# A retention and gated-convolution kernel: a loop in code and rotating tile pools, and one written list of small steps on fixed buffers

## Chip, cores and metric

The kernel runs on one core of a Trainium2 chip. The metric is the device time in microseconds (us). TensorE (PE) multiplies, VectorE (DVE), ScalarE (ACT) and GpSimd (POOL) work on tiles, SyncE (SP) issues the transfers. Each engine takes its instructions in the order in which the program gives them. TensorE writes into PSUM, eight banks of 512 float32 columns on 128 partitions.

## The reference, cut to what matters

```python
# q, k, v: (8, 8, 576, 64): batch, heads, tokens, head size; float32
scores = q @ k.T / 8                         # per batch and head
ret = scores * gamma[h] ** (i - j) where i >= j, else 0
x = (ret @ v), heads side by side            # (8, 576, 512)
gate_pre[t] = sum over kk of conv_w[kk] * x[t - 4 + kk]   # 5 taps per channel, causal
gate = 1 / (1 + exp(-gate_pre))
val = x @ w_val                              # 512 x 512
out = (gate * val) @ w_out                   # 512 x 512
```

## The kernel before

The decay factors out: k-side tokens are weighted with gamma^-j by multiplying v (`gin`), query tokens with gamma^i and the 1/8 when x is taken (`gout`). Causality is then a plain mask, and what earlier tokens give to later ones is a 64x64 state per head, which is carried.

The 576 tokens of a batch are cut into two units of 256 (two chunks c of 128 tokens) and a rest of 64; the rests of four batches make one unit more. That gives 18 units (`units`, L69), the last two being the rests. A partition holds two neighbouring tokens (r = 2). Per unit, in the names of the code:

- `load` (L97) brings k, q and v in quarter-megabyte halves by SP, in runs of 512 bytes; four buffers each. `cast1` (L212) makes bf16 on POOL (in the first units also on ACT and DVE) and weights v.
- `turn` (L231) transposes k and q, 16 transposes of 128x128 on TensorE, and `take_turn` (L248) copies them to SBUF on ACT.
- `scores` (L259) makes k q^T in two halves of 16 matmuls, each on a 64x64 part of the array (`QUAD`, L76, names the four parts), and `masks` (L273) multiplies by the mask on DVE.
- `carried` (L294) adds state times q, `values` (L322) adds v times masked scores, in the same two banks; `take_x` (L334) multiplies by `gout` into `xg` on DVE.
- `update` (L353) makes k^T v for the state, ACT copies it, and POOL adds it up (L378 to L394).
- `conv` (L417) does the five taps as 40 matmuls of 64x64 diagonal blocks by 256 tokens, in two banks; `gates` (L431) is the sigmoid on ACT.
- `value` (L440) does x w_val, 16 matmuls of 128x128 by 256 tokens, and `gated` (L450) multiplies by the gate on DVE.
- `project` (L456) does z w_out, 8 matmuls of 512 columns; ACT copies; `store` (L466) writes out by SP.

The order is written by hand from L490 to L609 for the units 0 to 3, with dummy matmuls (`warm`, L204) between; from L610 on, one loop does unit n's attention and unit n-1's convolution, values and projection:

```python
scores(n, 0); masks(n, 0)
conv(n - 1, 0)
carried(n, 0)
scores(n, 1, lambda: carried(n, 1)); masks(n, 1)
gate_values(n - 1, 0); gate_values(n - 1, 1)
values(n, 1); values(n, 0); take_x(n)
update(n + 1); cast(n + 2); turn(n + 1, ps_a)
take_turn(n + 1, 0); take_turn(n + 1, 1)
rows_out(n - 1)
```

Buffers come from pools that rotate. PSUM has four pools of two banks: `ps_a` (turns, convolution), `ps_s` (scores, update), `ps_o` (carried and values), `ps_v` (values of x, projection).

Of the kernel before, what the change touches and what calls it, by code (L numbers as in the profile page):

```python
# [16 lines left out]
PSUM = bass.MemoryType.PSUM  # L18


@with_exitstack
def kernel(
# [16 lines left out]
    NCH = S // P  # L39
    TAIL = S - NCH * P  # L40
    PAD = KC - 1
    GB = 4
    LA = 6
    W = 2 * P
    NC2 = S // W
    assert D == 64 and DM == H * D and TAIL == 64 and B % GB == 0 and NP == 4
    scale = 1.0 / math.sqrt(D)
    lng = [math.log(1.0 - 2.0 ** (-5.0 - h)) for h in range(H)]

    consts = ctx.enter_context(tc.tile_pool(name="c", bufs=1))  # L50
    lead = consts.tile([P, 96], F32, name="lead")
    ldp = ctx.enter_context(tc.tile_pool(name="ld", bufs=4))
    bfp = ctx.enter_context(tc.tile_pool(name="bfp", bufs=3))
    tp_sb = ctx.enter_context(tc.tile_pool(name="tsb", bufs=2))
    pp = ctx.enter_context(tc.tile_pool(name="pp", bufs=1))
    gp = ctx.enter_context(tc.tile_pool(name="gp", bufs=1))
    zp = ctx.enter_context(tc.tile_pool(name="zp", bufs=2))
    op_sb = ctx.enter_context(tc.tile_pool(name="osb", bufs=2))
    stp = ctx.enter_context(tc.tile_pool(name="stp", bufs=2))
    xp = ctx.enter_context(tc.tile_pool(name="xp", bufs=1))  # L60
    small = ctx.enter_context(tc.tile_pool(name="small", bufs=1))
    ps_a = ctx.enter_context(tc.tile_pool(name="psa", bufs=1, space=PSUM))
    ps_s = ctx.enter_context(tc.tile_pool(name="pss", bufs=1, space=PSUM))
    ps_o = ctx.enter_context(tc.tile_pool(name="pso", bufs=1, space=PSUM))
    ps_v = ctx.enter_context(tc.tile_pool(name="psv", bufs=2, space=PSUM))
# [5 lines left out]
    NU = len(units)  # L71

    jobs = [(u,) for u in range(NU)]
    lo, hi = slice(0, 64), slice(64, 128)
    half = (lo, hi)
    QUAD = ((0, 0), (1, 1), (0, 1), (1, 0))  # L76

    with tc.manual_schedule():

        loaded = {}  # L80
        SRC = {"k": k, "q": q, "v": v}

        def load1(n, u):
            kind, b, c = units[u]
            src = SRC[n]
            t = ldp.tile([P, H, 2 * D], F32, name=f"f{n}c")
            if kind == "full":
                for h0 in range(0, H, H // 2):
                    hs = slice(h0, h0 + H // 2)
                    nc.sync.dma_start(out=t[:, hs], in_=src[b, hs, c * W:(c + 1) * W, :].rearrange("h (p r) d -> p h (r d)", r=2))  # L90
            else:
                for i in range(GB):
                    nc.sync.dma_start(out=t[i * 32:(i + 1) * 32],
                                      in_=src[b + i, :, NC2 * W:S, :].rearrange("h (p r) d -> p h (r d)", r=2))
            loaded[n, u] = t

        def load(u):  # L97
            for n in "kqv":
                load1(n, u)

        nc.gpsimd.memset(lead[0:1, 0:1], 0.0)
        load(0)
        cwn = consts.tile([KC * NP, P], F32, name="cwn")
        nc.scalar.dma_start(out=cwn, in_=moe_conv_w.rearrange("k (o i) -> (k o) i", i=P))
        wvf = consts.tile([P, NP, DM], F32, name="wvf")
        wof = consts.tile([P, NP, DM], F32, name="wof")
        load(1)
        nc.sync.dma_start(out=wvf, in_=moe_w_val.rearrange("(o i) n -> i o n", i=P))
        wo_src = moe_w_out.rearrange("(pr ab hl p) n -> ab hl p pr n", pr=2, ab=2, hl=2)
        for (p0, blk, ab, hl) in ((0, 0, 0, 0), (64, 0, 1, 0), (0, 2, 1, 1), (64, 2, 0, 1)):  # L110
            nc.sync.dma_start(out=wof[p0:p0 + 64, blk:blk + 2, :], in_=wo_src[ab, hl])
        for u in range(2, 5):
            load(u)


        zero = consts.tile([P, 512], BF16, name="zero")
        nc.vector.memset(zero, 0.0)
        lsc = small.tile([P, 1], F32, name="lsc")
        lcol = small.tile([P, NP], F32, name="lcol")
        nc.vector.memset(lsc, math.log(scale))  # L120
        for h in range(H):
            nc.vector.memset(lcol[half[h % 2], h // 2:h // 2 + 1], lng[h])
        ident = small.tile([P, P], BF16, name="ident")
        nc.gpsimd.memset(ident, 1.0)
        nc.gpsimd.affine_select(ident, ident, pattern=[[-1, P]], base=0, channel_multiplier=1,
                                compare_op=ALU.is_equal, fill=0.0)
        identf = small.tile([32, 32], F32, name="identf")
        nc.vector.tensor_copy(identf, ident[0:32, 0:32])
        id2 = small.tile([P, 64], F32, name="id2")
        nc.vector.tensor_tensor(id2, ident[:, 0:64], ident[:, 64:128], op=ALU.add)  # L130

        posi = small.tile([P, S], mybir.dt.int32, name="posi")
        for c in range(2 * NC2):
            nc.gpsimd.iota(posi[:, c * P:(c + 1) * P].rearrange("p (r a) -> p r a", r=2), pattern=[[1, 2], [2, 64]],
                           base=c * P, channel_multiplier=0)
        nc.gpsimd.iota(posi[:, NC2 * W:S].rearrange("p (r a) -> p r a", r=2), pattern=[[1, 2], [2, 32]],
                       base=NC2 * W, channel_multiplier=0)
        toki = small.tile([P, NC2 + 1, 2], mybir.dt.int32, name="toki")
        nc.gpsimd.iota(toki[:, 0:NC2], pattern=[[W, NC2], [1, 2]], base=0, channel_multiplier=2)
        for i in range(GB):  # L140
            nc.gpsimd.iota(toki[i * 32:(i + 1) * 32, NC2, :], pattern=[[1, 2]], base=NC2 * W, channel_multiplier=2)
        gout = consts.tile([P, NP, S], F32, name="gout")

        def prep_gout(prs):
            for pr in prs:
                nc.scalar.activation(gout[:, pr, :], posi, AF.Exp, bias=lsc, scale=lcol[:, pr:pr + 1])

        tok = small.tile([P, NC2 + 1, 2], F32, name="tok")
        lrow = small.tile([P, H], F32, name="lrow")
        gin = small.tile([P, NC2 + 1, H, 2], F32, name="gin")  # L150
        for h in range(H):
            nc.vector.memset(lrow[:, h:h + 1], -lng[h])

        def prep_gin():
            nc.vector.tensor_copy(tok, toki)
            nc.vector.tensor_tensor(gin, tok.unsqueeze(2).to_broadcast([P, NC2 + 1, H, 2]),
                                    lrow.unsqueeze(1).unsqueeze(3).to_broadcast([P, NC2 + 1, H, 2]), op=ALU.mult)
            nc.scalar.activation(gin, gin, AF.Exp)


        mask = consts.tile([P, 2, P], BF16, name="mask")
        mask_h = consts.tile([P, 2, P], BF16, name="maskh")
        for (t, base) in ((mask, 0), (mask_h, P)):
            nc.gpsimd.memset(t, 1.0)
            nc.gpsimd.affine_select(t.rearrange("p j (r a) -> p j r a", r=2), t.rearrange("p j (r a) -> p j r a", r=2),
                                    pattern=[[-1, 2], [1, 2], [2, 64]], base=base, channel_multiplier=-2,
                                    compare_op=ALU.is_ge, fill=0.0)
        mask_t = consts.tile([P, 2, P], BF16, name="maskt")

        def prep_masks():  # L170
            nc.vector.tensor_copy(mask[hi], mask_h[hi])

        def prep_tail_mask():
            nc.vector.tensor_copy(mask_t, mask)
            for i in (0, 2):
                nc.vector.memset(mask_t[i * 32:i * 32 + 32].rearrange("p j (r a) -> p j r a", r=2)[:, :, :, 32:64], 0.0)

        xg = xp.tile([P, B, NP, PAD + S], BF16, name="xg")
        nc.gpsimd.memset(xg[:, :, :, 0:PAD], 0.0)

        wvb = consts.tile([P, NP, NP, P], BF16, name="wvb")
        wob = consts.tile([P, NP, DM], BF16, name="wob")
        dg = consts.tile([P, NP, KC, 64], BF16, name="dg")

        def prep_conv():
            cps = ps_a.tile([P, KC * NP], F32, name="a")
            nc.tensor.transpose(cps, cwn, identf[0:KC * NP, 0:KC * NP])
            cw = small.tile([P, KC * NP], F32, name="cw")
            nc.vector.tensor_copy(cw, cps)
            nc.vector.tensor_tensor(  # L190
                dg.rearrange("p o k j -> p k o j"),
                cw.rearrange("p (k o) -> p k o", o=NP).unsqueeze(3).to_broadcast([P, KC, NP, 64]),
# [473 lines left out]
```

## Time and profile before

| what | us |
|---|---|
| median of 3 runs (lowest, highest) | 168.03 (166.53, 168.66) |
| profiled execution, span from first to last instruction | 169.3 |
| busy PE, PE weight load, DVE, ACT, POOL in it | 150.8, 112.8, 99.6, 88.8, 98.4 |
| moved by DMA | 40.35 MB, mean 238 GB/s |

The profiled execution is one more execution; its span is its own time and lies 1.3 us above the median of the runs. In the slices of the profile the span is cut into 40 equal parts of 4.23 us, and a digit is the busy share in tenths; PEclk is the granted TensorE clock. In a chain line stand the start, the length, the engine and the line. In a group line stand the shape, the count, the busy us, the mean ns of one, and the idle time ahead of them with what ended it. Matmuls overlap in their pipeline, so the mean ns of a matmul is longer than the step from one to the next.

### The profile page before, as it was taken

To read this page: it belongs to the slowest core of one execution; us is meant where nothing else is said; L and a number is where in the kernel's file an instruction comes from. 1 tells how busy PE (TensorE), PEld (TensorE's weight loads), DVE (VectorE), ACT (ScalarE), POOL (GpSimd) and SP (SyncE) were. 2 spreads that over 40 slices of the span, in tenths; PEclk is the share of its full clock that TensorE was granted. 3 is DMA by queue.
4 is the path that set the end of the run, shared out by engine and by line. 5 is a ranking of instruction groups with operands and counts; after the bars stand their busy time and mean duration, and the time that the engine had idled before them with its cause. 6 is when DMAs were issued, how large, how long until landed. Compare 5 with 4: busy or idle time off the path is not lost.

```text
span 169.3 us, 7640 instructions
## 1 busy us (share of the span) xinstructions
PE 150.8 (89%) x3384; PEld 112.8 (67%) x3402; DVE 99.6 (59%) x153; ACT 88.8 (52%) x127; POOL 98.4 (58%) x123
## 2 busy tenths in 40 slices
PE   6677589978899979998999999999999999999960
PEld 2366456647678756877787776868787877868620
DVE  5684543475758481858383856658584938668330
ACT  6965330565273827382838374564838382654520
POOL 7565197157875846584849594956769499100000
PEclk9999755999999999999999999999999999999999
DMA  4999978999999999999999999787980311303125
GB/s 143 290 341 351 284 218 258 316 325 322 314 323 329 282 342 295 307 332 323 329 282 327 296 304 274 251 235 237 240 273 21 128 68 60 127 9 128 45 78 126
DMA packets 61071, 40.35 MB, mean 238 GB/s; under 512 B 2394, under 2 KB 57710, under 8 KB 61038
## 3 DMA queue, kind: packets, MB, share of 16 engines
q1 hardware_dynamic: 61008, 39.86, 77.7%
q8 instruction: 26, 0.43, 1.1%
q14 instruction: 7, 0.06, 0.1%
q10 hardware_dynamic: 30, 0.01, 0.0%
HBM read 30.42 MB, written 9.44 MB: 235 GB/s over the span
## 4 chain that ended last, share of the span: by engine, by line
PE 77%; DMA 5%; DVE 4%; issue 4%; POOL 4%; ACT 2%; SPq 1%; POOLq 0%; ACTq 0%; DVEq 0%
PE v L445 18%; PE v L461 17%; PE a L424 13%; PE a L246 8%; PE s L266 6%; PE o L330 6%; PE o L307 3%; DMA fqc<-in_q_dram 3%; PE s L367 2%; POOL vb L215 2%; DMA fkc<-in_k_dram 2%; DVE p L276 2%; SPq L90 1%; PE o L246 1%; DVE z L452 1%
## 5 line engine op out<-in xcount | busy, mean ns | idle before, releaser
L276 DVE TENSOR_TENSOR p<-s,mask 128x1024 bf16<-128x1024 f32 x28 | 34.3, 1224 | 40.2 <-PE s L266 40.2
L445 PE MATMUL v<-xg,wvb 128*128 128x256 bf16 x288 | 36.6, 281 | 0.5 <-DVE xg L341 0.5
L215 POOL TENSOR_TENSOR vb<-fvc,gin 128x1024 bf16<-128x1024 f32 x18 | 34.3, 1903 | 3.3 <-DMA fvc<-in_v_dram 3.3
L461 PE MATMUL v<-wob,z 128*128 128x512 bf16 x126 | 33.5, 380 | 1.3 <-DVE z L452 0.4
L249 ACT COPY kq<-a 128x1024 bf16<-128x1024 bf16 x28 | 27.0, 1015 | 10.0 <-PE a L246 10.0
L445 PEld LDWEIGHTS <-wvb 128*128 128x128 bf16 x288 | 27.3, 100 | 6.4 <-issue 1.4
L452 DVE TENSOR_TENSOR z<-gate,v 128x512 bf16<-128x512 f32 x36 | 24.6, 683 | 9.2 <-ACT gate L433 5.3
L433 ACT ACTIVATE gate<-a 128x1024 f32<-128x1024 f32 x18 | 18.4, 1024 | 16.1 <-PE a L424 9.1
L464 ACT COPY ob<-v 128x512 f32<-128x512 f32 x36 | 20.0, 605 | 9.6 <-PE v L461 9.6
L424 PE MATMUL a<-xg,dg 64*64 64x256 bf16 x720 | 24.2, 278 | 0.0
L375 ACT COPY xf<-s 128x512 f32<-128x512 f32 x12 | 7.0, 586 | 31.2 <-PE s L367 31.2
L341 DVE TENSOR_TENSOR xg<-o,gout 128x512 bf16<-128x512 f32 x32 | 22.2, 741 | 0.2
L461 PEld LDWEIGHTS <-z 128*128 128x128 bf16 x144 | 13.0, 98 | 13.6 <-DVE z L452 1.4
L424 PEld LDWEIGHTS <-dg 64*64 64x64 bf16 x720 | 20.5, 109 | 2.1 <-DVE xg L348 0.4
L266 PEld LDWEIGHTS <-kq 64*64 64x64 bf16 x576 | 13.5, 106 | 11.0 <-issue 10.0
L266 PE MATMUL s<-kq 64*64 64x128 bf16 x512 | 16.5, 223 | 3.2 <-issue 2.8
L389 POOL TENSOR_TENSOR mid<-run,xf 128x256 f32<-128x256 f32 x8 | 5.8, 727 | 20.3 <-ACT xf L375 14.2
L221 POOL CAST kb<-fkc 128x1024 bf16<-128x1024 f32 x16 | 16.6, 1039 | 0.2 <-DMA fkc<-in_k_dram 0.2
L221 POOL CAST qb<-fqc 128x1024 bf16<-128x1024 f32 x15 | 15.6, 1041 | 0.2 <-DMA fqc<-in_q_dram 0.2
L380 POOL CAST s<-xf 128x256 bf16<-128x256 f32 x8 | 3.2, 398 | 20.2 <-ACT xf L375 13.6
L330 PE MATMUL o<-p,vb 64*64 64x128 bf16 x576 | 12.6, 224 | 1.2 <-DVE p L276 1.2
L330 PEld LDWEIGHTS <-vb 64*64 64x64 bf16 x576 | 9.4, 109 | 5.3 <-issue 5.1
(75 smaller groups left out, 157.7 us busy)
## 6 DMA issues: line engine op xcount, KB each, us to landing
fkc<-in_k_dram SPq DMA_DIRECT2D x32, 256.0 KB, 5.1
fqc<-in_q_dram SPq DMA_DIRECT2D x32, 256.0 KB, 5.1
fvc<-in_v_dram SPq DMA_DIRECT2D x32, 256.0 KB, 5.1
out_dram<-ob SPq DMA_DIRECT2D x16, 512.0 KB, 4.8
wvf<-in_moe_w_val_dram SPq DMA_DIRECT2D x1, 1024.0 KB, 9.2
wof<-in_moe_w_out_dram SPq DMA_DIRECT2D x4, 256.0 KB, 10.0
fkc<-in_k_dram SPq DMA_DIRECT2D x8, 128.0 KB, 4.1
fqc<-in_q_dram SPq DMA_DIRECT2D x8, 128.0 KB, 4.5
```

The costliest lines, as they stand in the source:

```text
L215: nc.gpsimd.tensor_tensor(t.rearrange("p h r d -> p (h r) d"), loaded["v", u].rearrange("p h (r d) -> p (h r) d", r=2), gin[:, units[u][2] ...
L221: (eng or nc.gpsimd.tensor_copy)(t.rearrange("p r h d -> p h r d"), loaded[n, u].rearrange("p h (r d) -> p h r d", r=2))
L249: nc.scalar.copy(kqt[u][hf].rearrange("p i l r c a -> p i (l r c a)"), tps[u][:, :, hf].rearrange("p i l r a -> p i (l r a)"))
L266: nc.tensor.matmul(s[half[c], par, prl, r, :], lhsT=t[half[par], 0, prl, r, c, :], rhs=t[half[par], 1, prl, :, c, :], start=True, stop=Tru ...
L276: nc.vector.tensor_tensor(p.rearrange("p e l r a -> p (e l) (r a)"), sps[u, hf].rearrange("p e l r a -> p (e l) (r a)"), m.rearrange("p r ...
L330: nc.tensor.matmul(o[c][half[par], pr, :], lhsT=vb[half[c], 2 * pr + par, r, :], rhs=p[half[c], par, prl, r, :], start=first(u, c, par), s ...
L341: nc.vector.tensor_tensor(x[:, b, :, PAD + i0:PAD + i0 + P].rearrange("p o (a r) -> p o r a", r=2), o[c].rearrange("p o (r a) -> p o r a", ...
L424: nc.tensor.matmul(g[cols, bank, si, :], lhsT=dg[rows, blk, kk, :], rhs=xs(j, rows, blk, kk), start=(si == 0 and kk == 0), stop=(si == len ...
L445: nc.tensor.matmul(vp[:, si, :], lhsT=wvb[:, o, 2 * e + s, :], rhs=xs(j, slice(0, P), o, PAD), start=(si == 0 and o == 0), stop=(si == len ...
L452: nc.vector.tensor_tensor(zsb[j][:, 2 * e + ss[0]:2 * e + ss[-1] + 1, :], gsb[j, i][:, e], vps[j, i, e], op=ALU.mult)
L461: nc.tensor.matmul(o, lhsT=z[:, r, :], rhs=wob[:, jj, :], start=(jj == 0), stop=(jj == NP - 1))
L464: (eng or nc.scalar.copy)(outs[u][:, r], o)
```

## The change

The program becomes one list of 811 words, `ORDER`, which a last loop runs through; each word names a step, its unit or job, and its buffers or banks. There are no pools: every SBUF tile is a fixed buffer chosen by a number modulo its count, and PSUM is one tile of eight banks that the words name. The dummy matmuls shrink to three.

- Units stay; work behind x goes by jobs: units 0, 1, 16 and 17 alone, the others in pairs, so that `conv`, `sigmoid`, `value` and `gated` see 512 columns. `project` stays at one unit and one r.
- q is loaded per batch in halves of four heads (512 tokens, a partition holds four neighbouring tokens, runs of 1 KB; batch 0 by units). Tokens of a chunk then stand in the order of four, in q, masks, `gout` and x's PSUM columns.
- Turns work on row halves of 64 partitions and give 64 columns each.
- Convolution runs on 32x32 blocks, each row group into a bank of its own (four banks); the weights' rows and columns are laid out to match, and in odd pairs of heads the two halves of x's partitions change places.
- `carried` takes the tiles in an order in which four different parts of the array follow each other; there are no `fence` copies.
- Five buffers hold k and v (and in two of them first the weights), two hold q; three row buffers instead of two. The rests have their own x, `xt`, and `last_x` copies the four tokens that they need.
- Casts, copies and state steps name their engine in the list: 12 k casts, 6 q casts and 28 row copies go to ACT, 8 row copies and 8 turn copies to DVE, 45 of 48 state steps and 17 of 18 v casts to POOL.

The core of the diff:

```diff
+UNITS = [0, 1, 2, 3, 4, 5, 6, 7, 8, 9, 10, 11, 12, 13, 14, 15, 16, 17]
+JOBS = [(0,), (1,), (2, 3), (4, 5), (6, 7), (8, 9), (10, 11), (12, 13), (14, 15), (16,), (17,)]
+ORDER = """
...
+OC.4.0.0.6.A S.9.1.0.4 K.9.1.2 S.9.1.1.4 L.v.15.0 L.v.11.1 L.v.11.0 LQ.6.1 SS.9.2.P CK.11.2.P CQ.5.2.1.P CVV.11.2.P
+SS.10.1.P SS.10.0.P CQ.6.2.1.P PJ.4.1.1.7 PJ.4.0.1.6 X.8.0.0 X.8.1.0 M.9.1.4 PV.9.1.0.2 PV.9.0.0.2 K.9.0.2 PV.9.1.1.2
+PV.9.0.1.2 X.9.1.2 X.9.0.2 TK.10.0 TQ.5.2.4 OC.4.0.1.6.A OC.4.1.1.7.A TK.11.6 KT.10.0.A QT.5.1.5.A CV.5.0 QT.5.0.4.D
+KT.11.6.D SG.5.1.0 V.5.2.4 G.5.2.4 SG.5.0.0 S.10.1.0.6 K.10.1.2 S.10.1.1.6 M.10.1.6 S.10.0.1.4 S.10.0.0.4 M.10.0.4
...
+        def load_q(b, hh):
+            t = ldq[b % LOADQ].rearrange("p h r d -> p h (r d)")
+            nc.sync.dma_start(out=t[:, heads(hh)],
+                              in_=q[b, heads(hh), 0:NC2 * W, :].rearrange("h (p r) d -> p h (r d)", r=4))
...
+        def turn_k(i, b0):
+            ps = bank16[:, b0:b0 + 2].rearrange("p c (o r a) -> p c o r a", r=2, a=64)
+            for pr in range(NP):
                 for r in range(2):
+                    for c in range(2):
+                        nc.tensor.transpose(ps[:, c, pr, r, :],
+                                            kb[i % KBS][half[c], r, 2 * pr:2 * pr + 2, :].rearrange("p h d -> p (h d)"),
+                                            ident[half[c], half[c]])
...
+        def carried(i, odd, b0):
+            kind, b, cu = units[seq[i]]
+            for m in range(2):
+                for (prl, par) in ((0, 0), (1, 1), (1, 0), (0, 1)):
+                    pr, c, s = 2 * m + prl, par ^ odd, par ^ prl
                     rows = half[par]
+                    o = bank[half[s], b0 + c, pr * P:(pr + 1) * P]
...
+        def conv(j, b0):
+            n = cols(j)
+            for kk in range(KC):
+                for d in range(4):
+                    for rg in range(4):
+                        cg = (rg + d) % 4
+                        rows, cs = slice(32 * rg, 32 * rg + 32), slice(32 * cg, 32 * cg + 32)
+                        nc.tensor.matmul(bank[cs, b0 + rg, 0:n], lhsT=dg[rows, cg, kk, :], rhs=xs(j, rows, cg, kk),
+                                         start=(kk == 0), stop=(kk == KC - 1), skip_group_check=True)
...
+        def value(j, e, bk):
+            n = cols(j)
+            for o in range(NP):
+                nc.tensor.matmul(bank[:, bk, 0:n], lhsT=wvb[:, o, e, :], rhs=xs(j, slice(0, P), o, PAD),
+                                 start=(o == 0), stop=(o == NP - 1), skip_group_check=True)
...
+        for word in ORDER:
+            name, *args = word.split(".")
+            run[name](*args)
```

The words of the list are: L, LQ, LQ1, LQT, LV, LO, LC load k and v, q, and the weights; CK, CQ, CVV cast; TK and TQ turn, KT and QT copy the turns; S scores, M masks, K carried, PV weighted sums, X takes x; U update, XF its copy, SS the state's three steps; CV convolution, SG sigmoid, V values, G gating, PJ projection, OC its copy, ST store; XP copies the last tokens for the rests; words with z are set-up. A last letter A, D or P names the engine.

## The prediction

> **What bounds the kernel now.** I read the page's slices first, then the busy times by stretches of ten microseconds, then the chain that ended last, then the groups of instructions. The slices show two regimes.
>
> ```profile
> PE   6677589978899979998999999999999999999960
> DVE  5684543475758481858383856658584938668330
> PEclk9999755999999999999999999999999999999999
> DMA  4999978999999999999999999787980311303125
> ```
>
> Up to slice 11 (about 46 us) TensorE has holes and a stretch at half the granted clock; behind it TensorE is full to the last two slices. The DMA engines are full nearly from the start to about 105 us. The stretches say the same in numbers (busy us of PE, PEld, DVE, ACT and POOL, then granted clock, DMA share, GB/s):
>
> ```profile
> 20.00:30.00 10.00, 8.96 (x108) 6.22 (x108) 4.28 (x7) 3.06 (x7) 8.75 (x11) 0.55 0.87 252
> 40.00:50.00 10.00, 8.89 (x244) 6.69 (x245) 6.16 (x11) 5.21 (x11) 6.98 (x10) 1.00 1.05 323
> 90.00:100.00 10.00, 9.95 (x254) 7.77 (x254) 6.25 (x7) 6.34 (x9) 7.92 (x10) 1.00 1.03 311
> 100.00:110.00 10.00, 9.95 (x230) 7.94 (x227) 6.61 (x8) 5.54 (x7) 7.42 (x7) 1.00 0.85 269
> ```
>
> A busy TensorE alone proves little, so the chain decides. One turn of the steady loop, start and length in us:
>
> ```profile
> 95.34 0.28 PE s L367 x32
> 95.62 1.00 PE a L246 x16
> 96.62 0.22 PE v L461
> 96.89 1.46 PE v L461 x6
> 98.34 0.35 PE s L266 x16
> 98.69 1.23 PE a L424 x40
> 99.92 0.22 PE o L307 x4
> 100.46 0.17 PE s L266 x6
> 100.62 1.85 PE v L445 x16
> 102.48 0.57 PE o L330 x32
> 103.05 0.28 PE s L367 x32
> ```
>
> Nothing but TensorE stands in it: one unit costs 103.05 - 95.34 = 7.71 us. By starts: update 0.28, turns 1.00, projection 1.72, half of the scores 0.35, convolution 1.23, carried states with the other half of the scores 0.70 (so carried alone 0.35), values 1.85, weighted sums 0.57. Here TensorE work removed is time removed, until another engine takes over. The groups give the second in line, and three prices:
>
> ```profile
> L276 DVE TENSOR_TENSOR p<-s,mask 128x1024 bf16<-128x1024 f32 x28 | 34.3, 1224 | 40.2 <-PE s L266 40.2
> L452 DVE TENSOR_TENSOR z<-gate,v 128x512 bf16<-128x512 f32 x36 | 24.6, 683 | 9.2 <-ACT gate L433 5.3
> L341 DVE TENSOR_TENSOR xg<-o,gout 128x512 bf16<-128x512 f32 x32 | 22.2, 741 | 0.2
> ```
>
> DVE's masks wait for the scores, not the scores for the masks.
>
> **The change part by part**, per unit of 256 tokens, on TensorE.
>
> Convolution: 40 matmuls of 64x64 by 256 columns become 80 of 32x32 by 512 for two units. With four tiles abreast, 40 x 256 columns are 2560 column times in 1.23 us. With sixteen abreast, two units need 5 x 512 = 2560, so 1.23 us for two, 0.62 for one: 0.61 saved. Bounds: 0.35 (80 weight-and-matmul pairs for two units at the update's pace, 0.28 us / 32 = 8.75 ns, the fastest row) and 2.46 (still four abreast: 80 x 512 / 4 = 10240 columns for two units at 1.23 us per 2560, 4.9 us). I take 0.62, since the rows of 64x64 tiles run as wide as their array allows. For a job of one unit (four of them: 80 by 256 columns) I take half of the streaming and the same edge, 0.70, 0.53 saved.
>
> Against this speaks a rule of the Trainium skill, "TensorE: Matmul & The Clock Gate", Part 1: start to start never falls below about 25 ns. By it the 880 matmuls would take 22 us, as much as the old 18 x 1.23 = 22.1. The trace disagrees: L367 starts one per 8.75 ns.
>
> Turns: 16 transposes of 128 rows by 128 columns become 32 of 64 rows by 64 columns (16 for k, half of 32 for two units' q). If the two row halves run abreast, the columns in line fall from 2048 to 1024: 0.50. Bounds 0.28 (32 x 8.75 ns) and 2.00 (32 x 62.5 ns, each as long as now). I take 0.50, as L367 and L424 show both row halves at work together. Saved 0.50.
>
> Carried: the same 16 matmuls, but now four instead of two different tiles follow each other (the heads of odd pairs change halves). 0.35 becomes 0.18; bounds 0.14 (16 x 8.75) and 0.35. Saved 0.17.
>
> Values: 16 matmuls of 512 columns for two units instead of 32 of 256. Projection streams 512 columns in 1.72 / 8 = 215 ns, so 3.44 plus one edge of 0.14 for two, 1.78 for one: 0.07 saved. Bounds 1.72 and 1.85. Projection, scores, weighted sums and update keep their matmuls and tile sizes: nothing.
>
> Edges: each piece of the chain is 0.07 to 0.16 us longer than its columns need (weighted sums: 32 x 128 / 4 columns at the projection's 0.42 ns are 0.43, measured 0.57). The old loop changes tile size four times a unit, the list about 6.1 times from the turn of unit 4 on. 2.1 x 0.1 = 0.21 us lost per unit, bounds 0 and 0.34. Beside it stands the Trainium skill's "TensorEngine Tiling (Array Packing)", Key Properties, that a change of tiling mode drains the array; it gives no figure.
>
> Sum behind 46.5 us: turns 14 x 0.50 = 7.0, carried 14 x 0.17 = 2.4, convolution 13 x 0.61 + 2 x 0.53 = 9.0, values 13 x 0.07 = 0.9, edges -14 x 0.21 = -3.0. Together 16.3 us; a double unit's cost falls to 7.71 - 1.14 = 6.57.
>
> What lies beside. DVE keeps masks, gating and x: (34.3 + 4.9 + 4.9 + 24.6 + 22.2 + 3.0) / 18 = 5.2 us a unit. The list gives it 8 row copies, 8 turn copies and a few casts more, about 12 us or 0.7 a unit by the copies' rows (0.4 to 0.9 each). x is now written with a step of four elements; the step of two costs 741 - 683 = 58 ns over the plain write, so 0 to 58 more, twice a unit. 5.9 to 6.0 of 6.57: covered, but 90% full. If cover fails, at worst each unit waits for one mask, 1.22. ACT gains 12 k casts and 6 q casts (1.05 each, 19 us) and loses 16 copies: about 100 us in all, covered. POOL loses those casts (98.4 to about 87). Its queue reaches v sooner, which costs nothing.
>
> SP: q comes in halves of a batch, 1 KB runs instead of 512 B; about as many DMAs (some 140 for 150, about 0.5 us of issue each). Stores stand among loads in the list, so a store that waits for its copy holds the loads behind it; five key and value slots (four before) cover that by some 6 us each. Fixed banks: the convolution holds four of eight until two sigmoids of 1.02 are through, 3.2 us in 13.1 of a pair. The other four carry turns, scores and weighted sums; I price it at nothing, covered by the list's putting values behind it, at worst 1.02 per pair.
>
> Prologue (46.5 us): its own TensorE work falls by 4 x 0.50 + 3 x 0.35 x 0.5 + 2 x 0.53 + 0.61 = 4.2. The loads that units 0 to 3 and both weights need (about 8.4 MB) cross at about 30 us at the old pace, and half a dozen us of work follow: 36, so the gain is at most 10. At least 0: the dummy matmuls that hold the clock shrink from 41 to 3, and the chain could just wait longer for loads. I take 4.
>
> Total: 169.3 - 16.3 - 4 = 149.0 as a span. The page shows the span, 169.3, against a median of 168.03 for the three runs (166.53 to 168.66); less that 1.3 it is 147.7, say 148.
>
> **The rivals.** Differences within 2% count as no change: 164.7 to 171.4.
>
> The DMA engines take over. The stretches add to 32.8 MB by 110 us, always at a share near 1. In the new list all but seven quarter-megabyte loads, and eleven stores, stand before the store of unit 11: 30.4 - 1.8 + 5.8 = 34.4 MB, at that pace 115 us. Behind the last projection of job 6 TensorE still has six units of convolution, values and projection (4.12 each) and four of attention (2.2 each), 33.6, and the end takes 4: span 153, time 152. Against it: the weights' 2 KB runs brought slices 2 and 3 to 341 and 351 GB/s where the 512 B slices have 316 to 332, so q's 1 KB runs should help.
>
> DVE sets the pace. At 90% its order of masks, x and gating must fit TensorE's. Half of one mask lost per unit: 14 x 0.6 = 8, time 156. For: 90%; against: 40.2 us of idle time before masks now.
>
> A prologue at its lower bound, 36 us, with the steady sum reached: 148 - 6 = 142.
>
> The convolution is paced per instruction, not per column. Its old pace is 1.23 / 40 = 31 ns a matmul; 880 of these take 27 us where I have 7 x 1.23 + 4 x 0.70 = 11.4: 16 more, 164. Against: 8.75 ns of L367. By the skill's 25 ns floor, cited above, it would be 11 more, 159.
>
> On the other side: the sixteen tiles don't run abreast. With four abreast a double job takes 4.9 instead of 1.23 and a single one 2.5 instead of 0.70: 7 x 3.7 + 4 x 1.8 = 33 more, 181. It decides at 23 us more (171), near five abreast; with eight abreast it is about 10 more, 158. For it: no row shows 32x32 tiles. Against: 64x64 fills the array.
>
> **How the numbers follow.** Forecast 0.46 (its own range 143 to 154), DMA 0.17, DVE 0.13, short prologue 0.08: faster 0.84. Convolution per instruction: same 0.07. Four abreast: slower 0.09. The range leaves out these last two and little else: 139 to 162.
>
> **What would show it.** Right: 80 convolution matmuls of 512 columns in about 1.2 us; 16 turns in about 0.25; a pair of units in about 13.1; PE above 9 tenths behind 40 us. Wrong: PE waiting for DVE's masks or x, POOL or ACT casts waiting for loads behind 40 us, or a convolution of 2 us and more. A prologue longer than 46 us would undo the sum by itself.

## The result and the profile after

The changed kernel takes 187.08 us (median of 4 runs, 185.56 to 187.96); before, run beside it, 167.28 (4 runs, 166.24 to 168.66). The ratio is 1.116 (95% interval 1.105 to 1.126): slower by 11 to 13%, where 148.0 with a range of 139 to 162 was forecast. The profiled execution has a span of 185.0 us; it took 186.75, and in every run a time is about 1.7 us over its span. Ratios leave out runs more than 1.5% above the fastest of their kernel, the clearest being E1's profiled one, 203.64 us at a granted clock of 0.69.

The slices of the page:

```profile
PE   0256468897679896877899598889968985999880
DVE  4275596537944896889769768878791799797830
PEclk9999999999657999999999999999996999999998
DMA  5999999979798988768697899999978723000274
```

TensorE, at nine tenths in all but two of the slices 11 to 37 before, now has holes to the end; DVE stands at 6 to 9 in all but one of the slices 13 to 37, and the DMA engines are busy to the end of slice 31 (counted from 0), 148 us, where before they fell off at the end of slice 29, 127 us. Four stretches of the profile of after (busy us of PE, PEld, DVE, ACT, POOL, then granted clock, DMA share, GB/s):

```profile
20.00:30.00 10.00, 5.65 (x194) 4.11 (x187) 8.12 (x8) 3.41 (x8) 2.32 (x6) 1.00 1.13 266
50.00:60.00 10.00, 8.24 (x148) 4.20 (x148) 4.87 (x7) 6.01 (x7) 3.31 (x4) 0.62 0.94 280
80.00:90.00 10.00, 7.45 (x256) 4.66 (x255) 10.00 (x11) 4.15 (x5) 5.30 (x8) 1.00 0.73 223
100.00:110.00 10.00, 7.86 (x259) 4.80 (x258) 7.58 (x9) 5.61 (x8) 6.49 (x7) 1.00 0.93 286
```

From 80 to 90 us DVE is busy for all ten and TensorE for 7.45. The groups name what grew on DVE: the product that writes x, L341 before with 741 ns, is L463 now with 1369, on the same 128x512 elements.

```profile
L416 DVE TENSOR_TENSOR p<-bank,mask 128x1024 bf16<-128x1024 f32 x32 | 38.5, 1225 | 11.0 <-PE bank L410 8.6
L370 POOL TENSOR_TENSOR vb<-kv,gin 128x1024 bf16<-128x1024 f32 x17 | 32.3, 1902 | 28.3 <-DMA kv<-in_v_dram 25.3
L463 DVE TENSOR_TENSOR x<-bank,gout 128x512 bf16<-128x512 f32 x32 | 39.8, 1369 | 2.2 <-PE bank L454 2.0
```

The masks, behind 40.2 us of idle DVE before, now have 11.0 ahead of them. The timeline shows what that does to a pair's convolution (DVE first, then PE; start, length, and in brackets the idle time and who ended it):

```profile
81.46 2.35 DVE L416 TENSOR_TENSOR p<-bank,mask 128x1024 bf16<-128x1024 f32 x2
83.73 4.88 DVE L463 TENSOR_TENSOR x<-bank,gout 128x512 bf16<-128x512 f32 x4
...
87.49 0.64 PE L393 MATMUL bank<-ident,qb 64*128 64x64 bf16 x32 [1.37 <-DVE x L463]
88.67 1.35 PE L528 MATMUL bank<-x,dg 32*32 32x512 bf16 x80 [0.54 <-DVE x L463]
```

The list puts the four products of a pair in a row ahead of its convolution: 4.88 us in which DVE does nothing else, and TensorE waits twice at the end of it. The convolution itself takes what was forecast. The second place is the loads. From the chain of waits by engine, and then the DMA queue's own (us in total, times, longest):

```profile
POOL vb L370 <- DMA kv<-in_v_dram: 25.3, 7, 11.5
POOL qb L365 <- DMA lq<-in_q_dram: 9.6, 3, 6.7
POOL kb L360 <- DMA kv<-in_k_dram: 9.0, 2, 4.7
PE bank L528 <- DVE x L463: 7.8, 6, 2.1
...
SPq L254 <- DVE ob L552: 24.7, 3, 19.1
SPq L254 <- ACT ob L552: 19.9, 7, 6.3
SPq L203 <- ACT kb L360: 13.1, 4, 5.1
```

POOL waits for v, q and k; SP stands 44.6 us at stores (L254) that wait for their output copies, and 13.1 at loads whose slot is not yet cast.

**Three numbers for each kernel.** The starts of the pairs' convolutions split a span into the time to the first (prologue), six intervals of a pair, and the end. For the forecast's 149.0: six intervals of 13.1 and the end that the best kernel below has (26.3) leave 44.1 for the first.

| kernel | first pair's convolution | interval of a pair | end | span |
|---|---|---|---|---|
| forecast | 44.1 | 13.1 | 26.3 | 149.0 |
| after | 52.8 | 17.5 | 27.4 | 185.0 |
| E2, x walked in token order | 53.0 | 16.0 | 26.0 | 175.0 |
| E9, E2 without later loads | 52.6 | 14.7 | 26.5 | 167.0 |
| E12, E9 with early loads sooner | 47.0 | 14.8 | 26.3 | 162.0 |
| E15, all loads, more slots | 50.7 | 16.3 | 26.1 | 174.9 |

Of the 36.0 us that after's span is over 149.0, 8.7 lie ahead of the first pair's convolution, 26.2 in the six intervals, 1.1 at the end. In times the miss is 39.1: the time adds 1.7 to a span, and the forecast took 1.3 off its own. (By the same 1.7, before's profiled execution took about 171.0 us, 3 over the median and not 1.3; the forecast in time stays 147.7 either way.)

### The profile page after: what moved, and what is told of

It reads as the page before. It is cut to its first block, busy times and chain, and to the rows that moved or that the text cites. A ratio compares the mean times of both kernels' runs of the same rounds, so it can differ in the third digit from the quotient of the medians.

```text
span 185.0 us, 8224 instructions
## 1 busy us (share of the span) xinstructions
PE 141.9 (77%) x3700; PEld 83.5 (45%) x3700; DVE 130.2 (70%) x174; ACT 95.7 (52%) x129; POOL 81.9 (44%) x114
## 5 line engine op out<-in xcount | busy, mean ns | idle before, releaser
L416 DVE TENSOR_TENSOR p<-bank,mask 128x1024 bf16<-128x1024 f32 x32 | 38.5, 1225 | 11.0 <-PE bank L410 8.6
L370 POOL TENSOR_TENSOR vb<-kv,gin 128x1024 bf16<-128x1024 f32 x17 | 32.3, 1902 | 28.3 <-DMA kv<-in_v_dram 25.3
L463 DVE TENSOR_TENSOR x<-bank,gout 128x512 bf16<-128x512 f32 x32 | 39.8, 1369 | 2.2 <-PE bank L454 2.0
L543 DVE TENSOR_TENSOR z<-gate,bank 128x512 bf16<-128x512 f32 (+1 forms) x44 | 24.9, 587 | 21.3 <-PE bank L538 14.2
L548 PE MATMUL bank<-wob,z 128*128 128x512 bf16 x144 | 35.6, 380 | 0.9 <-DVE x L463 0.5
L538 PE MATMUL bank<-x,wvb 128*128 128x512 bf16 (+1 forms) x144 | 34.5, 387 | 1.1 <-DVE x L463 1.1
L533 ACT ACTIVATE gate<-bank 128x1024 f32<-128x1024 f32 (+1 forms) x22 | 17.9, 866 | 21.7 <-PE bank L528 21.7
L552 ACT COPY ob<-bank 128x512 f32<-128x512 f32 x28 | 16.2, 587 | 22.7 <-PE bank L548 21.0
L386 ACT COPY kt<-bank 128x1024 bf16<-128x1024 bf16 x15 | 15.1, 1013 | 13.7 <-PE bank L380 13.5
L410 PE MATMUL bank<-qt,kt 64*64 64x128 bf16 x576 | 18.5, 230 | 3.8 <-DVE kt L386 1.4
L528 PE MATMUL bank<-x,dg 32*32 32x512 bf16 (+1 forms) x720 | 14.7, 426 | 8.4 <-DVE x L463 7.8
L454 PE MATMUL bank<-p,vb 64*64 64x128 bf16 x576 | 16.4, 231 | 2.5 <-DVE p L416 2.3
```

The source lines that it names most:

```text
L370: TT[eng](vb[i % VBS][:, hs].rearrange("p h r d -> p (h r) d"), ldt[i % LOADS][:, 1, hs].rearrange("p h (r d) -> p (h r) d", r=2), gin[:, ...
L386: COPY[eng](kt[i % 2].rearrange("p o r c a -> p c (o r) a"), ps[:, :, 0:2 * NP])
L410: nc.tensor.matmul(s[half[c], par, prl, r, :], lhsT=kt[i % 2][half[par], pr, r, c, :], rhs=query(i)[half[par], pr, :, 32 * c:32 * c + 32], ...
L416: nc.vector.tensor_tensor(pt[i % 2][hf].rearrange("p e l r a -> p (e l) (r a)"), bank[:, b0:b0 + 2].rearrange("p e (l j) -> p (e l) j", l= ...
L454: nc.tensor.matmul(bank[half[s], b0 + c, pr * P:(pr + 1) * P], lhsT=vb[i % VBS][half[c], 2 * pr + par, r, :], rhs=pt[i % 2][hf][half[c], p ...
L463: nc.vector.tensor_tensor(xr[b % XS][:, :, PAD + i0:PAD + i0 + P].rearrange("p o (a r) -> p o r a", r=4), o, gout[:, :, i0:i0 + P].rearran ...
```

## The experiments

Times are medians, with those of before measured beside them and the ratio's 95% interval. Theory D: DVE sets the pace through the step of four in x. Theory L: late loads do. Rival T: TensorE's new shapes are slower than thought.

**E1, E2, E3: x written otherwise.** E1 writes x contiguously, with the token order left out. E2 gives the right order another way: the product walks in token order, so that the write is contiguous and the PSUM read steps by 32 columns. E3 lets the query copies group tokens by two, so that x has a step of two.

```diff
 E2
-  xr[...].rearrange("p o (a r) -> p o r a", r=4), o,
-  gout[...].rearrange("p o (r a) -> p o r a", r=4)
+  xr[...].rearrange("p o (a r) -> p o a r", r=4), o.rearrange("p o r a -> p o a r"),
+  gout[...].rearrange("p o (a r) -> p o a r", r=4)
```

> The changed kernel, but x is written one element after the other; the tokens of a chunk are not put back in order, so that step is left out. Theory X (the write in steps of four made each x product 1.37 us instead of 0.74; DVE is full and the convolution waits for four of these in a row): one product falls to about 0.69, a pair of units from 17.6 to about 15 us, the time from 187 to 165 to 172. Theory L (the list itself waits: its prologue, stores ahead of loads in SP's queue, pieces cut small): DVE gets idle time and the time stays above 180.

> The changed kernel, but the x product walks in token order: it writes one element after the other and reads PSUM in steps of 32 columns. If only the write minds steps, one product costs about 0.69 us and the time is as that of the kernel that leaves the order out (165 to 172 by theory X). If the read minds as much, the product stays near 1.37 us and the time near 187. Theory L: above 180 in both cases.

> The changed kernel, but the copies of the turned q put the tokens into the order of two, so that x is again written in steps of two, as before the change; each of the 18 copies becomes two of 512 columns. Theory X: the x product at 0.74 us as before, the copies at about 0.6 each, the time 167 to 175. Theory L: above 180.

E1 179.15, E2 176.24, E3 176.26 us, before 168.18; ratios 1.069 (1.062 to 1.077), 1.046 (1.035 to 1.057), 1.053 (1.045 to 1.061). The group of E2:

```profile
L463 DVE TENSOR_TENSOR x<-bank,gout 128x512 bf16<-128x512 f32 x32 | 20.5, 684 | 3.0 <-PE bank L454 2.8
```

The product takes 684 ns in E1 and E2, 750 in E3. The step is worth 187.1 - 176.2 = 11 us by E2 and E3 and 8 by E1, whose product is the same length; why E1 is 3 us slower than E2 is open. D is right for under a third of the miss, and not the whole: all three times lie above D's range for E1 (165 to 172) and under L's 180. The granted clock doesn't make the difference: runs of after at 0.960 to 0.978 took 185.6 to 188.0 us, runs of E2 at 0.970 to 0.984 took 174.1 to 177.0.

**E4: the same step in before.** x is written in steps of four in the old kernel.

> The kernel before with one thing of the change: x of the full units is written in steps of four (the tokens of a chunk land in a wrong order, since its PSUM order stays that of two). Both theories expect the product at about 1.37 us. If its cost lies on the path in any order of the work, 28 products of the steady loop at 0.63 more make 167 into 180 to 185. If it costs only where DVE is full (here 6.5 of 7.71 us a unit), the time stays within 2% of 167.

167.84 us (10 runs), before 168.18, ratio 0.999 (0.994 to 1.003). Two groups of E4:

```profile
L276 DVE TENSOR_TENSOR p<-s,mask 128x1024 bf16<-128x1024 f32 x28 | 34.3, 1225 | 22.3 <-PE s L266 22.3
L341 DVE TENSOR_TENSOR xg<-o,gout 128x512 bf16<-128x512 f32 x32 | 40.5, 1367 | 0.0
```

The product is as dear, 1367 ns, and costs nothing: DVE's idle time ahead of the masks falls from 40.2 to 22.3 and pays for it. There it runs two at a time, spread over the units; in these two kernels the price of the step comes out where DVE has no idle time beside it.

**E5, E6, E7: the loads of the prologue.** On E2: the weights in buffers of their own instead of slots 3 and 4 (E5); batch 0's q and half of w_val in loads over all 128 partitions instead of 64 or 32 (E6); both, with w_out in one load over 128 partitions, which puts its rows elsewhere (E7).

```diff
 E6
-LQ1.0.1.1 ... LQ1.0.1.0 ... LQ1.0.0.0 LQ1.0.0.1
+LQ.0.1 ... LQ.0.0
```

> The changed kernel with the x product in token order (176.2), and the two weights in buffers of their own instead of in two of the five key and value slots. Theory S (the loads of units 3 and 4 wait until the weights in their slots are cast, and that makes the first 53 us): the first pair's convolution starts 6 to 10 us sooner than at 53 us, the time falls to 166 to 170. Theory W (the loads are slow because pieces of 16 to 64 partitions are in flight): the transfers stay as slow, at most 3 us gained.

> The changed kernel with the x product in token order (176.2), but batch 0's q comes in two loads over 128 partitions instead of four over 64, and half of w_val in one over 128 instead of two over 64; w_out and the rests stay in pieces of 16 and 32. Theory W: the 512 byte packets of the first 20 us fall from 36 to 38 ns to about 30, the first pair's convolution starts 3 to 6 us sooner. Theory S: within 2 us of 176.

> The two edits together, and w_out also in one load over 128 partitions (its rows then stand elsewhere, so the products use the wrong rows of w_out). If S and W are both causes: convolution of the first pair at 40 to 43 us and a time of 161 to 166. If neither is, 174 and more: then the waits lie in the order of the list itself.

177.78 (177.24 to 178.3), 178.67 (175.62 to 179.88) and 174.09 us (170.74 to 175.21), before 167.99; the runs of E6 and E7 scatter too much for a ratio. Buffers alone give nothing. Loads over all partitions bring the first pair's convolution from 53.0 to 49.6 and, with both, 48.8; most of that is given back later (E7's span is 173.1, E2's 175.0). E6's start is as theory W had it, 3.4 us sooner, but not its time; E7 is far from the 40 to 43 that S and W together would have given.

**E8: pieces of 64 partitions, in before.** Two loads of a q unit take 64 partitions and 8 heads each, instead of 128 and 4.

> The kernel before, with each q load of a full unit as two over 64 partitions and eight heads instead of two over 128 partitions and four heads: same bytes, runs and number. Theory W: packets get longer, about 27.5 to 32 ns in the mean, and as the DMA engines are full here up to 105 us, the prologue grows and the time rises by 2 to 6 us. If pieces of 64 partitions cost nothing: within 1% of 167.5.

171.73 us against 167.99, ratio 1.027 (1.019 to 1.035). In the trace's packet records a 512 B packet takes 33.0 ns on average, 28.0 in before, though only q's loads, a third of the bytes, changed. So pieces of part of the partitions cost 2.7%. Which packets are slow the records don't say: half still take 27 ns, as before, and the mean rises through a quarter of them that take over 35. The loads of k, which are as before, land 6.4 us after issue instead of 5.1 (medians), but they share a queue with q's. After has 32.8 on average, 37 to 43 from 10 to 40 us, and 29.5 in the ten behind.

**E9: without the later loads.** E2 that loads only the first five key and value units and two batches of q, and uses them again.

> The changed kernel with the x product in token order (176.2), in which only the first five units' k and v, the first two batches' q and the weights are loaded; later units work on what lies in the buffers, and the rests' q is not loaded. Theory D (behind 53 us the loads come late, so casts, turns and update wait, and the pair takes 15.4 us): the pair falls to 13.1 to 13.8 and the time to 160 to 166; the first pair's convolution stays near 53 us. Theory O (the order of the list costs it, with loads in time too): 172 and more.

168.28 us (10 runs) against 168.36, ratio 1.005 (0.999 to 1.011): 8 less than E2, and between the two theories (160 to 166, and 172 and more). Pairs take 14.7, and the prologue is as long as ever. The later loads cost another 8 us, by their waits or by their traffic: E9 takes away both. Without either the kernel would still not have been faster, with this prologue.

**E10: stores on ACT's queue** instead of SP's, on E2.

> The changed kernel with the x product in token order (176.2), with the stores issued from ScalarE's queue instead of SP's, where they stand ahead of loads and wait for row copies (41 us of SP's waiting). Theory D1 (a waiting store holds the loads behind it, and that is why they are late): 169 to 173. Theory D2 (the loads are late because the transfers are slow, or because buffers come free late): within 2 us of 176, or worse by ScalarE's issues, 18 of about 0.5 us and 8 more for the rests.

198.37 us, ratio 1.187 (1.177 to 1.196). Neither theory: it is 22 us over E2. Now ACT stands at stores, and the masks' wait for scores grows from 15.6 us to 24.7; ACT's queue was not free to carry them. The loads don't come sooner either: POOL's wait for v is 26.8 us, in E2 25.9, though no store stands in SP's queue.

**E11: the old tile size in the convolution**, on E9: 40 matmuls of 64x64 by 512 columns for a pair.

> The kernel without the later loads, with the convolution in 40 matmuls of 64x64 by 512 columns per pair instead of 80 of 32x32 (wrong weights in one tap; the sums are not the reference's). One convolution of a pair grows from 1.28 to about 2.3 us, one of a single unit from 0.95 to about 1.2. If TensorE sets the pace when loads don't: 7 x 1.0 + 4 x 0.25 = 8 us more than that kernel. If another thing sets it: less than 3 more.

176.31 us, ratio 1.055 (1.043 to 1.067), 8.0 over E9. One pair's convolution in the timeline of E9, and then in that of E11:

```profile
66.55 1.35 PE L533 MATMUL bank<-x,dg 32*32 32x512 bf16 x80
```

```profile
67.42 2.36 PE L532 MATMUL bank<-x,dg 64*64 64x512 bf16 x40
```

A pair's convolution takes 2.35 us instead of 1.35: 7 x 1.0 + 4 x 0.3 for the single ones = 8.2, all of it in the time. T falls: in a pair the 32x32 tiles do gain what was forecast, and once x and loads are out of the way TensorE sets the pace.

**E12: E9 and E7 together.**

> E9 (x product in token order without the later loads, 168.28 us, first pair's convolution at 52.6) and E7 (weights in own buffers and in full-width loads, first pair's convolution at 48.8) in one. It leaves out the same loads as E9 (later units use the data of the first five, the rests' q is not loaded) and loads w_out's rows in another order, as E7. Theory that the wait ahead of the first pair's convolution and the steady part's late loads are two losses that add: the convolution starts at 48 to 49.5, the pairs take 14.5 to 14.8 as in E9, and the time is E9's less 3 to 4, 164 to 165.5 us. Rival, that TensorE's own work and its order in the list set both: pieces that the first pairs no longer wait for are waited for later, and the time stays within 1 of E9, 167.3 to 169.3. If the start falls below 46, more of it was loads than E7 showed and the time goes under 163.

162.02 us (8 runs) against 167.52, ratio 0.970 (0.965 to 0.975). The losses add, and by more than E7 gave and the expectation allowed (164 to 165.5): the first pair's convolution starts at 47.0 (at half the granted clock, as its 2.36 us show). Two of its stretches:

```profile
30.00:40.00 10.00, 9.01 (x269) 5.76 (x253) 6.48 (x11) 7.28 (x11) 8.10 (x12) 1.00 0.39 103
100.00:110.00 10.00, 9.73 (x304) 5.76 (x294) 7.85 (x11) 7.37 (x10) 6.02 (x7) 1.00 0.19 73
```

PE is back above nine tenths. It moves 19.4 MB instead of 40.4, so it is no version to use; it says what the list is worth with data in time.

**E13, E14, E15: why the later loads are late.** On E6, nothing left out: stores moved behind up to six of the loads that follow (E13); seven slots for five (E14); both (E15).

```diff
 E13                                   E14
-L.k.5.1 ST.1 ... L.k.7.0 L.k.6.0      -LOADS = 5
+L.k.5.1 ... L.k.7.0 ST.1 L.k.6.0      +LOADS = 7
```

> E6 (x product in token order, batch 0's q and half of w_val over 128 partitions, 175.6 to 179.9 us) with each store moved in the list behind up to six of the loads that follow it, never behind the copy that needs its buffer again. Nothing is left out. SP stood 38 to 45 us in all at stores that waited for their copies (19.1 us at one). Theory that this holds the loads: the waits of casts for loads fall by half, and half of the 8 us that the cut of the loads gave comes back, 170 to 173. Rival, slots: SP then stands at loads whose slot is not free, 175 to 179.

> E6 with seven key and value slots instead of five, the weights in slots 5 and 6, stores where the change has them. Nothing is left out. Theory that the stores hold the loads: a store that waits stops every load behind it however many slots are free, 175 to 179. Rival, slots: 170 to 173, and SP's waits for casts (13 us) are gone.

> Both of E13 and E14. Nothing is left out. If stores and slots hold the loads together, the time comes near the kernel without later loads and with early ones (162.0): 164 to 168, at or under before. If the transfers themselves are too slow (512 B pieces at 30 to 40 ns with 30 MB to move beside 9 MB of stores), the casts wait as long as in E6 and it stays at 172 to 178.

182.56, 176.65 and 178.39 us against 168.54; ratios 1.098 (1.079 to 1.116), 1.063 (1.044 to 1.082), 1.074 (1.049 to 1.100). E13 is slower than E6 and fits neither theory; E14 lies where the stores were to blame, E15 at the upper edge of slow transfers. None wins anything. In E15 the loads do come sooner: POOL's wait for v is 13.0 us (E2: 25.9), and SP's wait for casts of k falls from 13.1 us in after to 0.5 (at one load of q it now waits 8.9). The pairs still take 16.3, so that loads that come sooner did not give the time back. Another wait stands in their place: from 50 to 150 us TensorE is idle for 10.7 us in E15 with no releaser that the trace can name ("issue"), for 2.9 in E2 and 2.7 in E9. All ten such gaps over 0.3 us in E15 begin while a 16 KB packet of the queue that the page calls instruction (q8) moves, or within 1.1 us behind it; such stretches cover 38% of the span. That instructions come late there is a reading, and nothing here tests it.

**E16: the later loads moved, but into two spare buffers that nobody reads**, on E9.

> E9 (168.28 us) with the loads that it left out put back at their places in the list, but into two spare buffers that nothing reads; later units go on using the data of the first five, as in E9, so later units' data are not the reference's. Theory that the wait for loads costs the 8 us between E9 and E2: nobody waits, 167 to 170. Rival, that the traffic itself costs it (stores, instruction fetch and early loads slowed beside it): 173 to 177, as E2. Between the two both do.

199.22 us, ratio 1.203 (1.187 to 1.219): neither theory. Two spare buffers were too few, so that loads wait for earlier loads in SP's queue, with stores behind them. One such place in its timeline, SP, ACT and PE:

```profile
141.08 0.50 SPq L256 DMA_DIRECT2D out_dram<-ob  x1
...
145.11 1.07 ACT L554 COPY ob<-bank 128x512 f32<-128x512 f32 x2 [17.58 <-issue]
...
145.74 0.43 PE L412 MATMUL bank<-qt,kt 64*64 64x128 bf16 x8 [17.09 <-ACT ob L554]
```

A store goes out at 141, behind loads, and lands at 145.04; ACT copies into an output buffer at 145.11, after 17.58 us of standing (the trace names no releaser, the landing fits), and TensorE gets the bank back after 17.09. That is the whole way from a late store to TensorE, and two such gaps, 17.1 and 6.8 us of TensorE, are most of the loss. Four intervals hold no such gap; the middle two:

```profile
87.80:104.70 16.90, 14.80 (x411) 8.67 (x413) 11.38 (x15) 10.61 (x16) 9.86 (x11) 1.00 0.85 263
104.70:119.80 15.10, 13.25 (x372) 7.46 (x376) 11.78 (x16) 8.94 (x13) 7.15 (x9) 1.00 0.67 195
```

Where 227 and 195 GB/s move, they are 14.1 and 15.1 us, and 13.9 and 14.7 in E9. Where 263 and 284 move, they are 16.9 and 16.0, and 15.6 and 15.0 in E9: 1.3 and 1.0 us more, near the 1.35 by which E2's pairs, with 262 GB/s, exceed E9's. Nobody waits for these loads, so the traffic itself may be what the later loads cost; two intervals each don't settle it.

## Why the prediction was wrong

The step that failed first is the one on DVE: "the step of two costs 741 - 683 = 58 ns over the plain write, so 0 to 58 more" for the step of four. It measured 628 more (1369 - 741), eleven times the upper bound. In busy time, in which neighbours overlap a little, that is 39.8 - 22.2 = 17.6 us of DVE, with the rests' eight products (5.3 - 3.0) 20. DVE's 5.9 to 6.0 a unit becomes 7.0 to 7.1, over TensorE's forecast 6.57. A step of two bf16 still touches every 4-byte word; a step of four leaves every second one out, and no row of before showed such a write. The row was carried over a kink.

The Trainium skill, "Vector Engine (DVE) Microarchitecture Reference", section 5.2, has the rule, measured there on 4-byte elements: full rate needs runs of at least two adjacent 4-byte words, and a destination alone that steps by 24 words takes 2.50 ns a column instead of 1.05. From these figures an estimate is 512 x 1.45 = 740 ns more; measured over the contiguous write, 1369 - 684 = 685. Trace and rule agree within a tenth. "SBUF — State Buffer", in its note on cachelines, lets bf16 step up to 8 elements free, with two hits in 16 bytes; by that the step of four is free, and the 1369 ns speak against it.

Point by point, the other steps:

- **Convolution, right for pairs.** Forecast 1.23 for a pair and 0.70 for a unit; 1.28 to 1.35 and 0.95 to 1.01 by the trace, so a single unit costs 0.3 more, and E11 shows the gain in the time. The rivals "per instruction" and "four abreast" fall: 80 in 1.28 us is 16 ns each. The Trainium skill's floor of 25 ns between starts ("TensorE: Matmul & The Clock Gate", Part 1) would make 2.0 us; the trace disagrees for tiles abreast.
- **Carried and values, right; turns too low.** Eight carried take 0.11 to 0.12, eight values of 512 columns 1.83 (1.78). q's 32 turns for two units take 0.57 to 0.64 and k's 16 for one 0.36: 0.65 to 0.68 a unit where 0.50 was forecast.
- **Projection and scores "nothing", too low.** Counted from each matmul's start to the next, idle time left out, a pair of E12 has 3.8 us of projection, which the list cuts into pieces of four (3.44 forecast), 1.7 of scores (1.4), 1.2 of turns (1.0) and 1.44 of convolution (1.23; one of six ran at half the granted clock). TensorE's work is 14.1 us a pair against the 13.1, and its idle time 0.7 more: together the 14.8.
- **DMA price, wrong sign.** "q's 1 KB runs should help". In the packet records a 1 KB packet of after takes 46 ns at the median, less than two of 512 B at before's 27, but 57.9 on average, more than two of 28.0. At DMA shares of 1.13, 1.13 and 1.03 after moved 230, 266 and 242 GB/s in the three stretches from 10 to 40 us; before moved 323 at 1.09 and 316 at 1.09 in the first and the third. Loads of 64, 32 and 16 partitions are new there; E8 puts 2.7% on pieces of 64 in a kernel that is otherwise the old one.
- **SP "five slots cover that", wrong.** SP stands 44.6 us at stores. That a late store can reach TensorE is shown by E16, that the later loads cost 8 us by E9. Whether they cost it by coming late or by moving is open: in E15 they come sooner and nothing is won, and in E16 fast traffic that nobody waits for goes with longer pairs. The forecast had no term for either.
- **Prologue, "gain at most 10, at least 0", wrong.** "The chain could just wait longer for loads" was named and priced at nothing. It is 8.7 us longer than the forecast implied; E12 gets 5.6 of it back with full-width loads, buffers of their own for the weights, and no later loads among them.

The text on what would prove it wrong named three things, PE waiting for x, POOL's casts waiting for loads behind 40 us, and a prologue past 46 us. All three came. They were listed as single mishaps, with DVE at 0.13 and 156 us, and the chance of 0.09 for "slower" stood on another mechanism, tiles four abreast, that didn't come. What it lacked is that mishaps can add up. That one fixed order passes each late operation on to all engines is a reading that E4 fits, where the same dear product hides in the idle time of the old order; no run tests it alone.

Of the 39 us between 148.0 and 187.1, each taken on top of the one before: x's write 11 (E2), later loads 8 (E9), early loads 6 (E12; on E2, with the later loads in place, E7 gave 2), and 14 left. Of these, E12's trace puts 6 on TensorE's work (six pairs at 1.0), 4 on its idle time (six at 0.7) and 3 on the prologue (47.0 against 44.1); no run took them away.

## What to carry to other kernels

Price a new stride from a row with the same number of bytes between elements, not by drawing a line from a smaller step; where none exists, take a full extra pass as the upper bound (here 685 ns on 684), and measure it in one short kernel. Before an order that interleaves engines by hand replaces a looser one, write down each engine's idle time next to its hot operations: it is what paid for the dear product in E4, and the new order may have none. Keep loads over all partitions (E8). Where stores that wait share a queue with loads, measure before moving either: E10 and E13 moved the stores and lost.

## What the runs showed of the hardware

- DVE writing bf16 from an fp32 product of 512 columns: contiguous 684 ns, step of two 741 to 750, step of four 1367 to 1369. Reading PSUM in steps of 32 fp32 costs nothing (684 in E2, the same as E1's plain read).
- With a third of the bytes loaded into 64 of 128 partitions at a time, a 512 B packet takes 33.0 ns on average instead of 28.0, and the time rises by 2.7% (E8).
- Sixteen 32x32 tiles: 80 matmuls of 512 columns in 1.28 to 1.35 us.
- Stretches near half the granted clock came with TensorE occupied: 0.55 from 20 to 30 us in before, with PE busy for 8.96, and 0.62 from 50 to 60 us in after, with PE busy for 8.24, where a convolution took 2.37 us for 1.35.
- Of the 91 idle gaps of TensorE over 0.3 us, in all 18 profiles, for which the trace names no releaser, 81 begin while a packet of the instruction queue q8 moves or within 1.1 us behind it; of the 206 other gaps behind the first 20 us, 85 do. These stretches cover 33 to 40% of a span. It is a coincidence in time; a cause wasn't tested.
